# A recurrence and a routed mixture of experts: a newly searched order for five engines, smaller routing groups, and the sums of the first experts' inputs on VectorE

## The chip, the cores and the metric

One core of a Trainium2 chip. The metric is the device time of one execution in microseconds (us); lower is better. PE is TensorE, PEld its weight load, DVE is VectorE, ACT is ScalarE, POOL is GpSimd, SP is SyncE, which issues most of the DMAs.

## The reference

```
a_t  = exp(8 * sigmoid(r_gate) * log(clip(sigmoid(a_param))))
x_g  = sqrt(max(1 - a_t**2, 1e-6)) * sigmoid(i_gate) * x
h    = a_t[:, t] * h + x_g[:, t]            # over t, y[:, t] = h
tok  = y.reshape(20224, 256)
e    = argmax(tok @ w_gate)                 # 8 experts, w_gate 256 x 8
g    = softmax(tok @ w_gate)[e]
out  = g * (relu(tok @ w1[e]) @ w2[e])      # w1[e] 256 x 1024, w2[e] 1024 x 256
```

The inputs are 4 sequences of 5056 tokens of 256 channels, in float32.

## The kernel before

The 20224 tokens are 158 blocks of 128. Four blocks are a **quad**, of which there are 40 (the last has two blocks). The work of a quad is the **front**: `load` brings its gates and x (512 KB each), ACT computes `ti`, `th` (tanh), `ex` (exp), `sq` (square) and `rt` (square root), DVE computes `xi`, `b` and the recurrence `scan`. Tanh and exp on the one side and the square root on the other use different function tables of ACT, so a change of side costs a table load. Then come the **rows**: PE computes the gate logits (`lp`, `lt`) and transposes the quad to token rows (`yt`), DVE finds each row's largest magnitude (`am`) and its scale (`sc`), ACT and DVE write the row as two float16 halves (`hi`, `lw`).

Quads are put together in **groups** (`GROUPS`). Each group is routed at once: `r1` to `r6` on DVE with the two matmuls of `rk` on PE in the middle find the expert, the place of each token in its expert's stretch of a DRAM buffer, and the gate weight. `scat` on POOL writes each block there by an indirect DMA, after `fa` has put the gate weight and the token's number (`ids`) at the row's end. `fence` is a small DMA on SP behind the scatters of a group. After it the expert work is read back by `xl`: row ends (`meta`) and the transposed rows (`xT`).

The **expert work** is 90 slots, each of one expert and 256 tokens (the last 16 of 128). The first eight slots, one for each expert, are `raw`: their weights are still float32 and are prepared beside the work into float16 halves (`wm`, `wt`, `ws`, `wh`, `wl`) and written to a scratch buffer (`wr`). Their x needs the sum of its two halves: `join`, on POOL. For the first two (`PICK = 2`) x does not go through DRAM at all: DVE writes 0/1 selection matrices (`sel`) and PE gathers the rows by matmuls with them (`pick`), and ACT copies the result out (`xs`). The other 82 slots read float16 weights back (`w`, 1 MB each, left out where the expert is already in that buffer) and make six matmuls for a product in the first layer (`L1`) and three in the second (`L2`). Between lie `relu` (ACT) and `hl` (DVE). `ot` (ACT) scales the output with a factor from `fac` (POOL), and `store` (POOL) scatters it. Which expert a slot has is decided on the chip: after a group, `tab` on DVE deals out the full blocks of 256 to the next few slots.

Each engine runs its own list in order. The lists come from a planner in the same file (`Line`, `Plan`): every step is a task with an engine, an assumed duration, a priority, the tasks it follows and the buffers it takes; the planner plays them through and at each point takes the ready task of lowest priority. The priorities come from some fifteen numbers (`URGE`, `EARLY`, `PREP` and others), and `NUDGE` can add one for a single task (it is empty before).

Of the kernel before, what the change touches and what calls it, by code (L numbers as in the profile page):

```python
# [31 lines left out]
XMAX = 0.5  # L32
WTOP = 5.9e4


GROUPS = (2, 2, 2, 2, 1, 2, 3, 2, 1, 2, 2)
UNITS = 4
SINGLE = 6
BATCH = 2
PASSES = ((1, 256, 8),)  # L40

SPLIT = 8
FILL = (0.88, 0.95)
MARGIN = 1.0
LOW = 7
MOST = 6
# [7 lines left out]
PAIRS = 4  # L54
BLANK = 0
AHEAD = 8
# [3 lines left out]
PICK = 2  # L60

EARLY = 250.0

ELOAD = 90.0
WIDE = (3,)
FAR = 5.0
SWITCH = 42
PREP = (-46.0, -3.5, 112)

URGE = dict(quad=23.0, load=-22.0, norm=-37.0, rows=-11.5, hi=197.0, route=-208.0, scat=335.0, tab=-203.0,  # L70
            first=-850.0, slot=-3250.0, fac=-52.0, store=-90.0)
NUDGE = {}
BUFS = dict(r=3, i=4, x=6, rows=4, yt=2, lp=1, rank=1, tot=1, lg=4, hl=2, xT=4, hb=3, ot=9, po=1, p1=2, reg=3, x32=6)
# [8 lines left out]
class Line:  # L82

    LAT = 0.2

    def __init__(s):
        s.now, s.ids = 0.0, counter()
        s.engs = ("SP", "PE", "DVE", "ACT", "POOL")
        s.free = {e: 0.0 for e in s.engs}
        s.avail = {e: [] for e in s.engs}  # L90
        s.dma, s.act, s.calm = 0.0, "T", 0.0
        s.pools, s.uses, s.held = {}, {}, {}
        s.events, s.ops, s.made, s.done = [], [], 0, 0
# [69 lines left out]

    def run(s):
        heappush(s.events, (0.0, -1, None))
        while s.events:
# [5 lines left out]
            for e in s.engs:  # L172
# [3 lines left out]
                for k in s.avail[e]:  # L176
                    if k.ready > now + 1e-9 or not s.can_take(k.take) or k.name == "load" and s.early(*k.args):
                        continue
                    if k.name == "scat" and now < s.calm - 1e-9:
                        continue  # L180
                    p = (k.prio + (SWITCH if k.table and k.table != s.act else 0), k.seq)
# [8 lines left out]
                if k.table and k.table != s.act:  # L190
                    d += 1.3
                    s.act = k.table
                k.start = now
# [10 lines left out]
                elif k.size:  # L204
                    s.dma = max(s.dma, now + d + 0.6) + k.size
                    k.end = s.dma + 1.2
                else:
                    k.end = now + d
                heappush(s.events, (k.end, next(s.ids), k))
# [3 lines left out]
class Plan(Line):  # L213
# [14 lines left out]
    def build(s):  # L228
# [29 lines left out]
        T["blank"] = s.add("SP", 1.0, BLANK, "blank", size=7.0)  # L258
        for c in range(PASSES[0][0] + 1):
# [1156 lines left out]
```

## Time and profile before

| | us |
|---|---|
| median of three runs | 1052.61 (1051.04 to 1054.34) |
| profiled execution | 1058.75 |
| its span, first to last instruction | 1057.0 |
| PE busy in the span | 989.3 |
| DVE busy | 676.3 |
| ACT busy | 619.1 |
| POOL busy | 435.9 |

The busy time of an engine is the time in which at least one of its instructions runs; issuing a DMA is not counted for SP. [...]

### The profile page before, as it was taken

To read this page: it belongs to the slowest core of one execution; us is meant where nothing else is said; L and a number is where in the kernel's file an instruction comes from. 1 tells how busy PE (TensorE), PEld (TensorE's weight loads), DVE (VectorE), ACT (ScalarE), POOL (GpSimd) and SP (SyncE) were. 2 spreads that over 40 slices of the span, in tenths; PEclk is the share of its full clock that TensorE was granted. 3 is DMA by queue.
4 is the path that set the end of the run, shared out by engine and by line. 5 is a ranking of instruction groups with operands and counts; after the bars stand their busy time and mean duration, and the time that the engine had idled before them with its cause. 6 is when DMAs were issued, how large, how long until landed. Compare 5 with 4: busy or idle time off the path is not lost. (4 is left out here: it accounts for less than half of the span.)

```text
span 1057.0 us, 23781 instructions
## 1 busy us (share of the span) xinstructions
PE 989.3 (94%) x8854; PEld 862.1 (82%) x8854; DVE 676.3 (64%) x1387; ACT 619.1 (59%) x815; POOL 435.9 (41%) x522
## 2 busy tenths in 40 slices
PE   1469899999999999999999999999999999999997
PEld 1138688888888989888888888888888888889987
DVE  4998889887686565876847578466876473232211
ACT  8988685675746467567555765557666442222222
POOL 0264446434555335363452644525264434222222
PEclk9979899999999999999999999999999999999999
DMA  9967998899999979897899898999699994999790
GB/s 367 382 248 209 329 339 314 291 328 369 333 299 290 344 246 342 275 379 203 286 343 356 271 310 269 297 329 302 235 321 295 310 321 140 262 265 326 223 249 26
DMA packets 169347, 307.12 MB, mean 291 GB/s; under 512 B 117636, under 2 KB 122377, under 8 KB 147978
## 3 DMA queue, kind: packets, MB, share of 16 engines
q1 hardware_dynamic: 153770, 262.81, 78.4%
q0 software_dynamic: 15456, 42.74, 11.9%
q8 instruction: 70, 1.15, 0.5%
q14 instruction: 51, 0.42, 0.1%
HBM read 251.48 MB, written 65.30 MB: 300 GB/s over the span
## 5 line engine op out<-in xcount | busy, mean ns | idle before, releaser
L1129 PE MATMUL p<-xT,wt 128*128 128x256 f16 (+1 forms) x3936 | 413.6, 263 | 2.5 <-DMA wt<-wscr 2.2
L1129 PEld LDWEIGHTS <-wt 128*128 128x128 f16 x3936 | 354.9, 98 | 40.8 <-DMA wt<-wscr 2.5
L1193 POOL DMA_INDIRECT out<-ot,meta x164 | 181.1, 1104 | 400.2 <-ACT ot L1182 353.7
L1171 PE MATMUL po<-wt,hb 128*128 128x256 f16 x1184 | 322.9, 273 | 8.3 <-ACT ot L1182 6.4
L1149 DVE SCALAR_TENSOR_TENSOR hb<-p,hb 128x1024 f16<-128x1024 f32 x148 | 180.5, 1220 | 224.3 <-ACT hb L1141 207.2
L1173 PE MATMUL po<-wt,hb 128*128 128x256 f16 x1184 | 322.8, 273 | 0.1
L1172 PE MATMUL po<-wt,hb 128*128 128x256 f16 x1184 | 322.8, 273 | 0.1
L1141 ACT ACTIVATE hb<-p 128x1024 f16<-128x1024 f32 (+1 forms) x164 | 167.4, 1021 | 196.7 <-PE p L1129 167.8
L888 POOL DMA_INDIRECT buf<-rows,pi x158 | 172.4, 1091 | 47.8 <-issue 35.8
L1182 ACT ACTIVATE ot<-po,f 128x256 f32<-128x256 f32 x148 | 69.9, 472 | 172.7 <-PE po L1173 125.3
L1172 PEld LDWEIGHTS <-hb 128*128 128x128 f16 x1184 | 115.8, 98 | 21.7 <-issue 8.7
L1171 PEld LDWEIGHTS <-hb 128*128 128x128 f16 x1184 | 115.8, 98 | 16.6 <-issue 2.7
L1173 PEld LDWEIGHTS <-hb 128*128 128x128 f16 x1184 | 115.8, 98 | 13.7 <-issue 0.3
L699 DVE TENSOR_TENSOR_SCAN in_x<-in_r,in_x 128x512 f32<-128x512 f32 (+7 forms) x82 | 97.5, 1198 | 1.4
L680 DVE SCALAR_TENSOR_TENSOR in_x<-in_i,in_x 128x1024 f32<-128x1024 f32 (+1 forms) x38 | 45.7, 1203 | 48.8 <-ACT in_i L675 40.8
L1112 POOL TENSOR_SCALAR f<-meta,wt,wt 128x2 f32<-128x2 f32 (+1 forms) x82 | 37.5, 458 | 95.5 <-DMA wt<-wscr 76.6
L793 DVE SCALAR_TENSOR_TENSOR rows<-yt,fa,rows 128x256 f16<-128x256 f32 x154 | 65.4, 478 | 14.1 <-ACT rows L783 7.1
L783 ACT ACTIVATE rows<-yt,fa 128x256 f16<-128x256 f32 x154 | 61.8, 475 | 7.2 <-DVE fa L775 6.2
L1169 PE MATMUL po<-wt,hb 128*128 128x256 f32 x256 | 62.1, 392 | 1.5 <-ACT ot L1180 1.3
L664 DVE SCALAR_TENSOR_TENSOR in_x<-in_i,in_x 128x1024 f32<-128x1024 f32 (+1 forms) x38 | 46.2, 1221 | 23.5 <-ACT in_i L658 18.5
L1129 PE MATMUL p<-x,wt 128*128 128x256 f32 x256 | 59.3, 386 | 0.7 <-ACT x L928 0.7
L763 DVE TENSOR_REDUCE m<-yt 128x2 f32<-128x512 f32 x77 | 50.2, 678 | 11.2 <-PE yt L756 10.8
(126 smaller groups left out, 911.2 us busy)
## 6 DMA issues: line engine op xcount, KB each, us to landing
wt<-wscr SPq DMA_DIRECT2D x164, 1024.5 KB
in_x<-in_rix SPq DMA_DIRECT2D x39, 512.0 KB
in_r<-in_rix SPq DMA_DIRECT2D x37, 512.0 KB
in_i<-in_rix SPq DMA_DIRECT2D x37, 512.0 KB
wscr<-hl SPq DMA_DIRECT2D x16, 1024.5 KB
wt<-in_w SPq DMA_DIRECT2D x16, 1024.0 KB
buf<-pad SPq DMA_DIRECT2D x10, 272.0 KB
out<-ot,meta POOLq DMA_INDIRECT x164
```

Source lines behind the costliest of these rows:

```text
L699: V.tensor_tensor_scan(y[:, lo:hi], av[:, lo:hi], y[:, lo:hi], init, ALU.mult, ALU.add)
L793: V.scalar_tensor_tensor(r[:, 2 * p + j, D:2 * D], o["yt", p][:, j], o["sc"][:, 2 * p + j:2 * p + j + 1], r[:, 2 * p + j, 0:D], ALU.mult, ...
L888: i = G.indirect_dma_start(out=buf[:, :], out_offset=bass.IndirectOffsetOnAxis(ap=g["pi"][:, b0 + j:b0 + j + 1], axis=0), in_=rows[q]["row ...
L1129: T.matmul(pv[:, i], wv[:, wl, kk, fs], o["xT"][:, 2 * xl + kk, 0:U], start=(z == 0), stop=(z == len(seq) - 1))
L1141: A.activation(o["h"][:, gs, 0:U] if o["raw"] else o["h"][:, 0, gs, 0:U], o["p1", g], AF.Relu)
L1149: V.scalar_tensor_tensor(o["h"][:, 1, gs, 0:U], o["p1", g], 0.0, o["h"][:, 0, gs, 0:U], ALU.max, ALU.subtract)
L1169: T.matmul(dst, h[:, f, ts], wv[:, f, :], start=(f == 0), stop=(f == NF - 1))
L1171: T.matmul(dst, h[:, 0, f, ts], wv[:, 0, f, :], start=(f == 0), stop=False)
L1172: T.matmul(dst, h[:, 0, f, ts], wv[:, 1, f, :], start=False, stop=False)
L1173: T.matmul(dst, h[:, 1, f, ts], wv[:, 0, f, :], start=False, stop=(f == NF - 1))
L1182: A.activation(o["ot", j], o["po", j], AF.Copy, scale=o["f2"][:, j:j + 1])
L1193: i = G.indirect_dma_start(out=out[:, :], out_offset=bass.IndirectOffsetOnAxis(ap=o["id"][j], axis=0), in_=o["ot", j], in_offset=None, bou ...
```

## The change

The task's work is the same: 90 slots, of which 8 raw, 66 of 256 and 16 of 128 tokens. What changes:

- **The orders.** Most of the planner's numbers are new, its assumed durations are shorter, it now counts eight outstanding DMAs on each issuing queue and a slow PE at the start, and `NUDGE` has some 700 entries. So all five lists are in another order.
- **Groups.** The first groups are as before (two quads each), the later ones are of one quad: 31 groups instead of 21, and with them 31 routings and fences instead of 21, and 22 tables instead of 19.
- **One picked expert instead of two.** `sel` and the columns of `pick` are halved; seven raw slots go through DRAM and `join` instead of six.
- **`join` on DVE** instead of POOL.
- **Rows that are not picked** (quads 4 and up) scatter in blocks each led by two copies, the block's ids and its gate weights, where before two wider copies served the quad. The ids of the picked quads are copied by a task of their own (`tag`).
- The sum of `wt` alternates between two columns, `ws` uses one scale for each layer, the row buffer `inc` is held until its table is read.
- A raw slot whose weights would be read back (`BACK`) is added to the planner; with `PASSES` as it is no slot uses it.

```diff
-GROUPS = (2, 2, 2, 2, 1, 2, 3, 2, 1, 2, 2)
+GROUPS = (2, 2, 2, 2, 1, 2, 2, 1, 3, 2, 1)
-SINGLE = 6
-BATCH = 2
+SINGLE = 8
+BATCH = 1
-LOW = 7
-MOST = 6
+LOW = 9
+LOWS = 3
+MOST = 4
-BLANK = 0
-AHEAD = 8
+BLANK = 20
+AHEAD = 10
-PICK = 2
+PICK = 1
+ADDER = 'DVE'
-EARLY = 250.0
+EARLY = 580.4
-URGE = dict(quad=23.0, load=-22.0, norm=-37.0, rows=-11.5, hi=197.0, ...
+URGE = dict(quad=23.9, load=-21.4, norm=-91.8, rows=-18.2, hi=371.6, ...
-NUDGE = {}
+NUDGE = {
+"L1(0,0)": -172.8, "L1(0,1)": -110.6, "L1(1,0)": -22, ...
...
     @op
     def fa(q):
         g, b0, _ = group(q)
-        r, nb = rows[q]["rows"], plan.quads[q]
-        if plan.group_of[q] <= PASSES[0][0]:
-            for j in range(nb):
-                G.tensor_copy(r[:, j, D:D + 1], g["mx"][:, b0 + j:b0 + j + 1])
-            return
-        G.tensor_copy(r.bitcast(I32)[:, 0:nb, D + 1:PITCH], ids[:, q * QB:q * QB + nb]...)
-        G.tensor_copy(r[:, 0:nb, D:D + 1], g["mx"][:, b0:b0 + nb].unsqueeze(2))
+        for j in range(plan.quads[q]):
+            G.tensor_copy(rows[q]["rows"][:, j, D:D + 1], g["mx"][:, b0 + j:b0 + j + 1])
...
     @op
     def scat(q, j):
         g, b0, _ = group(q)
         c = plan.group_of[q]
+        if not plan.picked(q):
+            mark(q, j)
+            G.tensor_copy(rows[q]["rows"][:, j, D:D + 1], g["mx"][:, b0 + j:b0 + j + 1])
         i = G.indirect_dma_start(
...
     def join(k):
-        G.tensor_tensor(x[:, :, 0:U], o["xT"][:, 0:2, 0:U], o["xT"][:, 2:4, 0:U], ALU.add)
+            (V if ADDER == "DVE" else G).tensor_tensor(x[:, :, 0:U], o["xT"][:, 0:2, 0:U], ...)
```

ACT, from the second pair of quads' square roots to the copy of the picked x (line 928 before, 1411 after); `hb` and `in_i` are gates, `rows` the float16 rows. Before:

```order
L675 ACT_TABLE_LOAD
L675 ACTIVATE hb<-hb,quarter 128x1024
L653 ACT_TABLE_LOAD
L653 ACTIVATE hb<-hb,k_89 128x512
L669 ACTIVATE hb<-hb 128x1024
L675 ACT_TABLE_LOAD
L675 ACTIVATE hb<-hb,quarter 128x1024
L647 ACT_TABLE_LOAD
```

After:

```order
L1138 ACTIVATE hb<-hb 128x1024
L1144 ACT_TABLE_LOAD
L1144 ACTIVATE hb<-hb,quarter 128x1024
L1138 ACTIVATE hb<-hb 128x1024
L1144 ACTIVATE hb<-hb,quarter 128x1024
L1261 ACTIVATE rows<-yt,fa 128x256 x4
L1127 ACT_TABLE_LOAD
```

The two square roots of the pair stand together, with two table loads around them instead of four; ahead of the copy of the picked x ACT's list has 13 table loads before and 8 after.

DVE, behind the second group's routing (buffers numbered; `in_x` are fronts, `hl` weights in preparation, `m` magnitudes). Before:

```order
L680 SCALAR_TENSOR_TENSOR in_x_193<-in_i_190,in_x_193 128x1024
L988 SCALAR_TENSOR_TENSOR hl_573<-misc_131,wtop_121 128x2
L990 RECIPROCAL wsc_695<-hl_573 128x1
L699 SCALAR_TENSOR_TENSOR in_x_193<-in_r_231,in_x_168,in_x_193 128x512
L699 SCALAR_TENSOR_TENSOR in_x_193<-in_r_231,in_x_193 128x512
L664 SCALAR_TENSOR_TENSOR in_x_297<-in_i_204,in_x_297 128x1024
L1000 SCALAR_TENSOR_TENSOR hl_573<-wt01_137,wsc_695,hl_573 128x2048
L763 TENSOR_REDUCE m_744<-yt_705 128x2
```

After, up to the first `join` (line 1599):

```order
L1487 SCALAR_TENSOR_TENSOR hl_609<-wt10_141,wsc_661,hl_609 128x2048
L1133 SCALAR_TENSOR_TENSOR in_x_399<-in_i_422,in_x_399 128x1024
L1133 SCALAR_TENSOR_TENSOR in_x_701<-in_i_447,in_x_701 128x1024
L1475 SCALAR_TENSOR_TENSOR hl_698<-misc_133,wtop_121 128x2
L1477 RECIPROCAL wsc_747<-hl_698 128x1
L1242 TENSOR_REDUCE m_750<-yt_740 128x2
L1133 SCALAR_TENSOR_TENSOR in_x_513<-in_i_672,in_x_513 128x1024
L1242 TENSOR_REDUCE m_750<-yt_753 128x2
L1487 SCALAR_TENSOR_TENSOR hl_698<-wt00_138,wsc_747,hl_698 128x2048
L1133 SCALAR_TENSOR_TENSOR in_x_487<-in_i_694,in_x_487 128x1024
L1599 TENSOR_TENSOR x32_782<-xT_737 128x512
```

The sum for the second expert now stands in DVE's list behind fronts, rows and weight operations; before, it stood on POOL behind the scatters.

POOL, the scatter of a quad that is not picked (ids, gate weights, indirect DMA). Before:

```order
L881 COPY rows<-ids 128x4x15
L882 COPY rows<-mx 128x4
L888 DMA buf<-rows,pi 166400x272
L1193 DMA out<-ot,meta 20224x256
L888 DMA buf<-rows,pi 166400x272 x3
```

After:

```order
L1349 COPY rows<-ids 128x15
L1369 COPY rows<-mx 128x1
L1370 DMA buf<-rows,pi 166400x272
L1695 DMA out<-ot,meta 20224x256
L1349 COPY rows<-ids 128x15
L1369 COPY rows<-mx 128x1
L1370 DMA buf<-rows,pi 166400x272
```

Each block now has its own two copies; 142 blocks are scattered so.

## Rows read from the trace of the kernel before

**Rows 1.** The page's part 1: busy us (share of the span) xinstructions.

```profile
PE 989.3 (94%) x8854; PEld 862.1 (82%) x8854; DVE 676.3 (64%) x1387; ACT 619.1 (59%) x815; POOL 435.9 (41%) x522
```

**Rows 2.** Windows: from:to, length, busy PE PEld DVE ACT POOL, clock, DMA share, GB/s.

```profile
0.00:80.00 80.00, 32.97 (x176) 16.57 (x176) 61.39 (x153) 71.59 (x84) 26.62 (x49) 0.91 0.89 334
80.00:205.00 125.00, 120.28 (x610) 102.23 (x611) 109.80 (x173) 93.32 (x107) 60.92 (x55) 0.97 0.90 292
205.00:350.00 145.00, 139.08 (x1257) 120.97 (x1256) 109.52 (x242) 88.63 (x123) 71.31 (x81) 1.00 1.03 328
350.00:800.00 450.00, 449.39 (x4187) 398.17 (x4186) 306.68 (x640) 280.51 (x380) 199.43 (x234) 1.00 0.93 298
800.00:1000.00 200.00, 198.99 (x2034) 179.36 (x2032) 79.11 (x175) 72.09 (x104) 64.43 (x87) 1.00 0.88 268
1000.00:1057.00 57.00, 48.55 (x601) 44.76 (x598) 9.80 (x8) 12.92 (x18) 13.19 (x19) 0.95 0.54 151
```

**Rows 3.** Timeline of PE: start, us, line, operation [idle before, releaser].

```profile
76.13 3.62 PE L922 MATMUL p<-hb,rows 128*128 128x512 f16 x16
...
80.42 3.72 PE L1129 MATMUL p<-x,wt 128*128 128x256 f32 x16 [0.67 <-ACT x L928]
...
205.14 2.78 PE L1129 MATMUL p<-xT,wt 128*128 128x256 f16 x24
...
1027.82 4.44 PE L1129 MATMUL p<-xT,wt 128*128 128x128 f16 x48 [2.18 <-DMA wt<-wscr]
```

**Rows 4.** Timeline of ACT ahead of the first expert's matmuls.

```profile
76.54 1.28 ACT L658 ACT_TABLE_LOAD   x1
...
79.79 1.07 ACT L928 COPY x<-p 128x512 f32<-128x512 f32 x2 [0.89 <-PE p L922]
```

**Rows 5.** Timeline of DVE: end of the second group's routing, first selection.

```profile
69.14 0.20 DVE L871 RECIPROCAL mx<-mx 128x8 f32<-128x8 f32 x1
69.26 3.40 DVE L910 TENSOR_SCALAR hb<-cst,pf 128x256 f16<-128x256 f16 x16
```

**Rows 6.** Timeline of POOL and SP: last early scatter, fence, first join.

```profile
84.58 0.97 POOL L888 DMA_INDIRECT buf<-rows,pi  x1 [0.30 <-issue]
...
90.84 0.25 SPq L933 DMA_DIRECT2D fence<-buf  x1
...
96.06 1.16 POOL L1100 TENSOR_TENSOR x<-xT 128x512 f32<-128x512 f16 x1 [10.51 <-DMA xT<-buf]
```

**Rows 7.** Timelines of DVE and POOL: one weight operation twice, and a join.

```profile
76.09 2.33 DVE L1000 SCALAR_TENSOR_TENSOR hl<-wt,wsc,hl 128x2048 f16<-128x2048 f32 x1
...
98.11 3.27 DVE L1000 SCALAR_TENSOR_TENSOR hl<-wt,wsc,hl 128x2048 f16<-128x2048 f32 x1
98.08 1.15 POOL L1100 TENSOR_TENSOR x<-xT 128x512 f32<-128x512 f16 x1 [0.86 <-DMA xT<-buf]
```

**Rows 8.** Timeline of POOL: the same four copies at two places.

```profile
69.40 0.72 POOL L879 COPY rows<-mx 128x1 f32<-128x1 f32 x4 [6.91 <-DVE mx L871]
...
75.69 3.91 POOL L879 COPY rows<-mx 128x1 f32<-128x1 f32 x4
```

**Rows 9.** POOL's groups by line and form: id copies (busy us, mean ns).

```profile
L881 POOL COPY rows<-ids 128x60 int32<-128x60 int32 x35 | 13.6, 388 | 0.0
...
L786 POOL COPY rows<-ids 128x15 int32<-128x15 int32 x16 | 4.5, 326 | 8.2 <-DMA ids<-in_ids 8.2
```

**Rows 10.** DVE's groups by line and form: two operations.

```profile
L819 DVE TENSOR_TENSOR oh<-eq,pmx 128x64 f16<-128x64 f32 x17 | 8.5, 502 | 0.6
...
L664 DVE SCALAR_TENSOR_TENSOR in_x<-in_i,in_x 128x512 f32<-128x512 f32 x1 | 0.7, 691 | 0.7 <-ACT in_i L658 0.7
```

**Rows 11.** Windows in the first experts' stage, columns as above.

```profile
125.00:130.00 5.00, 3.48 (x12) 2.80 (x13) 4.83 (x11) 2.71 (x3) 0.00 (x0) 0.66 1.04 370
130.00:135.00 5.00, 5.00 (x18) 3.99 (x17) 4.33 (x8) 3.53 (x4) 0.98 (x1) 0.65 0.99 352
```

**Rows 12.** Waits of PE from 205 to 400 us: total us, times, longest.

```profile
PE po L1171 <- ACT ot L1182: 4.1, 3, 2.2
```

More of the change, by code (lines that the diff above doesn't have):

```diff
@@ L258, in build @@
         T["blank"] = s.add("SP", 1.0, BLANK, "blank", size=7.0)
+        s.parts, e = [], 0
+        for c, U, n in PASSES:
+            s.parts.append((c, U, list(range(e, e + n))))
+            e += n
         for c in range(PASSES[0][0] + 1):
@@ L370, in route @@
+        T["r3", c] = a("DVE", 0.58 * f, pr, "r3", c, after=[T["rk", c]], take=[("inc", c)], give=[("rank", c)])
+        T["r4", c] = a("DVE", 0.2 * f, pr, "r4", c, after=[T["r3", c]])
+        T["gt", c] = a("ACT", 0.2 * f, pr - 6, "gt", c, after=[T["r1", c]], table="T")
+        T["r5", c] = a("DVE", (0.45 if c <= PASSES[0][0] else 0.3) * f, pr, "r5", c, after=[T["r4", c]])
+        T["r6", c] = a("DVE", 0.7 * f, pr, "r6", c, after=[T["gt", c], T["r5", c]] + [T["sc", q] for q in g])
         sc = []
@@ L391, in route, with fenced @@
                 for k in range(PICK):
-                    T["xs", k] = a("ACT", 0.55, -210 + k, "xs", k, after=[T["pick", q]], take=[("x32", k)], give=[("p1", "pick")])
+                    T["xs", k] = a("ACT", 0.18 + 0.32 * PASSES[0][1] / 256, -210 + k, "xs", k, after=[T["pick", q]], take=[("x32", k)], give=[("p1", "pick")])
+    def fenced(s, c):
+        s.routed(c)
+        s.add("DVE", 0.01, -1e6, "drop", c, after=[s.tabbed], give=[("inc", c)])
     def routed(s, c):
@@ L432, in table @@
         k0 = len(s.slots)
[L433 to L435 removed]
+        x = s.tabbed
+        for j, d in enumerate((0.9, 0.85, 0.95)):
+            x = s.tabbed = s.add("DVE", d, pr, "tab", z, j, after=[x])
         new = []
@@ L1094, in join, with add, weights @@
     @op
+    def add(k):
+        o = slots[k]
+        x, o["xT"] = o["xT"], ps_y.tile([P, 2, D], F32, name="yt")
+        for l in range(2):
+            T.matmul(o["xT"], id16, x[:, 2 * l:2 * l + 2], start=(l == 0), stop=(l == 1))
+    @op
     def join(k):
         o = slots[k]
-        U = o["U"]
         x = work.tile([P, 2, 256], F32, name="x32", bufs=BUFS["x32"])
-        G.tensor_tensor(x[:, :, 0:U], o["xT"][:, 0:2, 0:U], o["xT"][:, 2:4, 0:U], ALU.add)
+        if ADDER == "PE":
+            A.copy(x, o["xT"])
+        else:
+            U = o["U"]
+            (V if ADDER == "DVE" else G).tensor_tensor(x[:, :, 0:U], o["xT"][:, 0:2, 0:U], o["xT"][:, 2:4, 0:U], ALU.add)
         o["xT"] = x
+    def weights(o, i):
+        return o.get("head", o)["w", i]
     @op
```

302 lines of the change are left out of this document (179 added, 123 removed), and 412 rows, old and new, of the table NUDGE.

## The prediction

> **What bounds the kernel now.** I read the busy times first, then the span cut into stages, then the list of PE at the borders of the stages, and last what PE waited for. PE is busy 989.3 of 1057.0 us [rows 1], so the time is PE's work plus the time in which PE has none. The stages [rows 2] show where that is. From 0 to 80 us PE works 33.0 us: the reader is to see that here ACT is the full engine, 71.6 of 80, and that DVE has 61.4. From 80 to 205 us, the eight float32 experts, PE has 120.3 of 125 and DVE 109.8, so DVE is a close second. From 205 to 350 us PE lacks 5.9 us while the DMA share is 1.03; from 350 to 1000 us it lacks 1.6 us of 650; in the last 57 us it lacks 8.5, of which some 4.3 follow the last matmul. The first expert's matmuls begin at 80.42 us, the first float16 ones at 205.14 [rows 3]. So there is not much to gain: the start, about 8 us within the first experts (idle and a slow clock), and about 12 us of gaps behind them.
>
> The executed work of the experts is the same: both lists hold 164 first-layer groups, the same float16 matmuls and 164 weight loads. With the reference's inputs the tables need 16 of the last small slots in both, so the conditional code for more is not entered.
>
> **The change part by part.**
>
> *The start.* ACT's list up to the copy of the picked x has 13 table loads before and 8 after, at 1.28 us each [rows 4]: 6.4 us. It has two operations over 1024 elements fewer ahead of it; two copies of 512 elements take 1.07 [rows 4], so about 2.1, and one copy instead of two, 0.5. That is 9.0 us off an engine that is busy 71.6 of the first 80 [rows 2]. On the other engines: behind the second routing, which ends at 69.34, DVE selects for 3.40 us [rows 5]; halved, that saves 1.7. The last 16 matmuls of the pick take 3.62 [rows 3]; halved in columns, 1.8. Routing to first matmul goes from 11.1 us to about 7.6. Bounds: if only this chain is shorter, 3.5 us; if ACT's 9.0 come off and its 8.4 us of waiting go as well, 17. The quads' inputs come through the same busy DMA (share 0.89 [rows 2]) behind six 1 MB weight loads, as before, so I keep a little back from the 9.0 and take **-8**: first expert at 72.4, second routing done near 64.8.
>
> *One picked expert instead of two.* Before, two experts (four times 3.72 us each by [rows 3], 30 us together) covered the way of the others through DRAM: last scatter at 84.58, fence at 90.84, first join at 96.06 [rows 6], 26.7 us behind the routing's end at 69.34 [rows 5]. Now one expert, 14.9 us and some 2 us of PE's other rows, must do it. 72.4 + 17 = 89.4; 64.8 + 26.7 + 0.7 for the join = 92.2. The scatters could be quicker, since the eight weight copies stand ahead of them in one piece. DVE's own queue ahead of the first join holds three weight operations of 2.33 [rows 7], six operations over 1024 elements and six over 512 at 0.69 [rows 10] for each 512, and small ones: about 23 us, which ends at 88 if it never waits, so the DMA way ends last. PE idles 0 to 8 us there; I take **+2**.
>
> *`join` on DVE.* Seven times 0.69 by the nearest row, an operation on 512 elements with two inputs [rows 10], is 4.8 us for DVE. But POOL's join had a price on DVE too: the same weight operation took 2.33 us alone and 3.27 with a join beside it [rows 7]. Six times 0.94 is 5.6. So I cost the move at **0** (bounds -6 and +5 us of DVE, whose spare time of 15 us in the stage [rows 2] hides it). [...]
>
> *Copies before each scatter.* 35 quads had one id copy of 0.388 [rows 9] and one of the weights; 142 blocks now have an id copy of 0.326 (the narrow form, [rows 9]) and a weight copy that takes 0.18 to 0.98, four in 0.72 or in 3.91 us [rows 8]. POOL's extra work is 50 us at the low price, and 160 us if every copy takes 0.98. POOL is busy 435.9 us [rows 1] and becomes 46 to 56% busy. What hides it: a 256-token slot takes PE 10.3 us, 96 matmuls of the 4187 in 450 us [rows 2], and in that time POOL has two stores, a factor and about two blocks. A block is 1.3 for the DMA and 0.5 to 2 for the copies. So I take **0**, and keep the upper end for the last rival.
>
> *Smaller groups.* Ten more routings of 13 small DVE operations, none dearer than 0.50 [rows 10]: under 65 us, nearer 30, and three more tables. They lie behind 205 us, where DVE is idle 35, 143 and 121 us in the three stages [rows 2]. On PE ten more pairs of matmuls with at most 64 columns; 512 columns cost 0.23 [rows 3], so 0.06 to 0.23 each: **+1**.
>
> *The orders behind 205 us.* PE waits there for ACT's output copy, at most 2.2 us at a time [rows 12], and that copy waits for a factor which needs the weights; DMA is full (1.03). Of the weight loads 30 are left out before, and by the same tables 22 now; eight more are 8 MB, 26 us of DMA at 328 GB/s [rows 2] spread over a run whose share is about 0.93. At the end a wait for weights costs 2.18 us, and the matmuls behind it run slow, 4.44 us [rows 3]. Of 11.6 us of such gaps a new order can remove all, or add some 6 more. One wait ends as another begins on a full DMA, so I take a third: **-4**. [...]
>
> The sum is -8 + 2 + 0 + 0 + 1 - 4 = -9. Against the profiled execution, 1058.75, that is 1049.75. The profiled one lay 6.1 us above the median of the runs, so against the median the forecast is 1052.61 - 9 = **1043.6 us**.
>
> **The rivals.** A difference under 0.3% (3.2 us) can't be told from none.
>
> 1. *The new order closes nearly all gaps.* PE's row from 205 to 1000 us is already almost full, which speaks for a list that can be kept full; that the DMA is full where PE waits speaks against it. Then -8, nothing for the second expert, -7 in the first experts, -11.6 behind, +1: -25.6, 1027 us.
> 2. *The start is given back.* DVE has 109.8 us of work in the first experts' stage and its list begins only some 4.5 us earlier (64.8 against 69.34), with seven joins more. If its waits, 15 us, stay, the float16 experts begin at 203 to 206 as before, and PE idles in between. Then the time is within 3 us of 1052.
> 3. *POOL's copies and DVE block each other (slower).* Six quads, 24 blocks, are scattered in the first experts' stage: 48 copies where 12 stood. At 0.33 us of DVE held per copy that is 16 us, and at 0.98 us per copy POOL's eight blocks of a group take 27 us instead of 11, so fence and tables come later. DVE's 15 us of spare time are gone from some 8 us of holding on, if it still waits as it does; from there each us goes to PE, which loses the 8 of the start and 7 more. Time 1060. For it: [rows 7, 8]. Against it: four copies beside the selection took only 0.72. [...]
>
> **How the numbers follow.** The forecast has 0.48, no gaps 0.20, given back 0.16, slower 0.16. Faster by over 0.3% is the first two, 0.68; no difference 0.16; slower 0.16. The range reaches from the full case without gaps, 1027, to within the slow one, 1058, which leaves out less than 2 in 10; the likeliest case alone is 1036 to 1049, by the bounds of the start and of the second expert.
>
> **What would show it.** In the new profile: the first expert's matmul at 69 to 76 us, 8 table loads ahead of it, a pick of half the length; PE idle for about 2 us before the second expert; the first float16 matmul near 197; ACT's share of the first 80 us no longer the largest by far. DVE's weight operation should not be stretched by a join any more, but may be by copies. PE should lack 6 to 9 us from 205 us to the last matmul. I am wrong if the first expert begins at 78 or later, if PE idles over 8 us before the second one, if the float16 work begins past 203, or if PE waits for stores or factors on POOL.

## The result and the profile after

The changed kernel takes 1063.17 us (median of four runs, 1061.44 to 1065.59) where the kernel before takes 1052.73 in the same comparison: ratio 1.0101, 95% interval 1.0074 to 1.0128. It is about 1% slower, 10.4 us, where I had forecast 9 us faster. Its profiled execution took 1065.59 us with a span of 1063.7, 6.7 us longer than the span before.

The page's part 1 of the kernel after answers to [rows 1]:

```profile
PE 989.3 (93%) x8874; PEld 869.0 (82%) x8874; DVE 693.6 (65%) x1561; ACT 617.4 (58%) x822; POOL 465.0 (44%) x726
```

PE is busy as long as before to a tenth, so the difference of the spans equals that of PE's idle time. That the two busy times agree is chance: the pick has become 7.8 us shorter (below), and the other matmuls together take as much longer. The windows of the kernel after, cut and laid out as [rows 2], say where it lies:

```profile
0.00:80.00 80.00, 33.84 (x206) 25.36 (x207) 62.23 (x144) 71.34 (x83) 26.25 (x52) 0.87 0.97 356
80.00:205.00 125.00, 113.24 (x578) 94.76 (x577) 107.36 (x180) 94.37 (x109) 46.64 (x65) 0.96 0.93 294
205.00:350.00 145.00, 139.92 (x1227) 122.06 (x1226) 112.49 (x252) 94.55 (x130) 81.43 (x126) 0.99 1.04 328
350.00:800.00 450.00, 448.42 (x4197) 396.05 (x4195) 340.46 (x863) 284.80 (x402) 233.71 (x366) 1.00 1.01 316
800.00:1000.00 200.00, 200.00 (x2019) 180.94 (x2017) 60.04 (x116) 57.93 (x82) 62.91 (x100) 1.00 0.90 259
1000.00:1063.70 63.70, 53.92 (x661) 49.84 (x658) 11.03 (x9) 14.43 (x20) 14.04 (x20) 0.94 0.49 143
```

Length less PE's busy time, stage by stage, before and after: 47.0 and 46.2; **4.7 and 11.8**; 5.9 and 5.1; 0.6 and 1.6; 1.0 and 0.0; 8.5 and 9.8. The sums are 67.7 and 74.4. In these two executions the stage from 80 to 205 us, the first experts, has taken all of it; what other executions show of the stages behind it stands under "Why the prediction was wrong". PE's timeline of the kernel after shows that stage, as [rows 3] did (at the end of a row: the idle time ahead of it, and what ended it):

```profile
71.92 8.86 PE L1631 MATMUL p<-x,wt 128*128 128x256 f32 x32 [2.55 <-ACT x L1411]
...
88.72 5.41 PE L1671 MATMUL po<-wt,hb 128*128 128x256 f32 x16 [2.03 <-ACT ot L1682]
93.97 3.62 PE L1631 MATMUL p<-x,wt 128*128 128x256 f32 x16
...
102.78 3.72 PE L1671 MATMUL po<-wt,hb 128*128 128x256 f32 x16 [1.46 <-ACT hb L1643]
108.16 1.99 PE L1671 MATMUL po<-wt,hb 128*128 128x256 f32 x8 [1.66 <-ACT ot L1684]
...
140.02 5.38 PE L1631 MATMUL p<-x,wt 128*128 128x256 f32 x16 [2.12 <-DMA wt<-in_w]
...
198.46 0.63 PE L1225 MATMUL yt<-cst,in_x 128*128 128x128 f32 x4 [2.13 <-DVE rows L1268]
...
206.03 2.78 PE L1631 MATMUL p<-xT,wt 128*128 128x256 f16 x24
```

The first expert does begin 8.5 us earlier, at 71.92 against 80.42. The second (93.97) needs no wait for its x. In between and behind, PE stops for 1.5 to 2.1 us again and again: for ACT's output copy, for the relu, for weights, for rows. Behind the waits at 88.72 and 140.02 the next 16 matmuls take 5.4 instead of 3.72 us, which is another 1.7: the granted TensorE clock, as a share of full speed, is 0.83 in the windows from 90 to 100 and from 140 to 150 us. Behind the two shorter ones, 1.46 and 1.66 us, they do not. The float16 work begins at 206.03, 0.9 us later than before.

And it begins with more left to do. PE's groups by line and form from 0 to 205 us, before:

```profile
L1129 PE MATMUL p<-x,wt 128*128 128x256 f32 x256 | 59.3, 386 | 0.7 <-ACT x L928 0.7
L1169 PE MATMUL po<-wt,hb 128*128 128x256 f32 x224 | 54.7, 394 | 1.5 <-ACT ot L1180 1.3 <-ACT ot L1182 0.2
```

and after:

```profile
L1631 PE MATMUL p<-x,wt 128*128 128x256 f32 x256 | 61.3, 397 | 4.7 <-ACT x L1411 2.5 <-DMA wt<-in_w 2.1
L1671 PE MATMUL po<-wt,hb 128*128 128x256 f32 x204 | 49.8, 396 | 6.4 <-ACT ot L1684 2.9 <-ACT ot L1682 2.0 <-ACT hb L1643 1.5
L1404 PE MATMUL p<-hb,rows 128*128 128x256 f16 x64 | 12.2, 375 | 6.0 <-DVE hb L1392 6.0
```

The pick is down from 20.0 us (486 ns for 512 columns before) to 12.2. But of the float32 matmuls of the experts 480 were done by 205 us before and 460 are now: 20 more at 0.22 us (7.17 for 32, as PE's timeline has it undisturbed) are still to come, 4.4 us. Counting these matmuls at several moments gives the course of the lead: at 90 us 35 before and 54 after, 19 ahead; at 112 us 126 and 130, 4 ahead; at 205 us 20 behind. So nearly all of the lead of 8.5 us is gone by 112 us, within the second expert. From there to 205 us another 24 matmuls, some 5 us, are lost; PE idles 6.6 of these 93 us, 3.4 before. The groups from 70 to 112 us in the kernel after show where it went:

```profile
L1631 PE MATMUL p<-x,wt 128*128 128x256 f32 x74 | 18.5, 409 | 2.5 <-ACT x L1411 2.5
L1671 PE MATMUL po<-wt,hb 128*128 128x256 f32 x56 | 14.8, 422 | 5.1 <-ACT ot L1682 2.0 <-ACT ot L1684 1.7 <-ACT hb L1643 1.5
```

Behind the first expert's start these are 5.1 us of waits and 3.4 us of slow matmuls (8.86 instead of 7.17 and 5.41 instead of 3.72). Before, one wait of 0.88 us stood there, in PE's timeline:

```profile
108.84 1.99 PE L1169 MATMUL po<-wt,hb 128*128 128x256 f32 x8 [0.88 <-ACT ot L1180]
```

That is 7.6 us more, of a lead of 8.5. (The slow matmuls are in part this execution's own: join_gpsimd has the same wait of 2.55 us ahead of its first expert, and then 7.17, not 8.86.)

The end has changed its wait, but has not become cheaper: from 1000 us on PE idles 9.8 us, 8.5 before. PE's timeline of the kernel after at 1020 us, to be read beside the last of [rows 3]:

```profile
1019.52 0.61 PE L1631 MATMUL p<-xT,wt 128*128 128x128 f16 x8 [0.30 <-PEq L1821]
1023.90 4.42 PE L1631 MATMUL p<-xT,wt 128*128 128x128 f16 x40 [3.77 <-issue]
```

The wait for weights, 2.18 us, is gone. In its place PE stands still for 3.77 us in the middle of a group, eight matmuls behind a branch (line 1821, around the code for more small slots), and waits for nothing that the profile shows. The 40 matmuls behind it run slow, 4.42 us; the granted clock is 0.62 from 1025 to 1030 us.

### The profile page after: what moved, and what is told of

The parts are those of the page before. It is cut to its first block, busy times and chain, and to the rows that moved or that the text cites. A ratio compares the mean times of both kernels' runs of the same rounds, so it can differ in the third digit from the quotient of the medians.

```text
span 1063.7 us, 24237 instructions
## 1 busy us (share of the span) xinstructions
PE 989.3 (93%) x8874; PEld 869.0 (82%) x8874; DVE 693.6 (65%) x1561; ACT 617.4 (58%) x822; POOL 465.0 (44%) x726
## 3 DMA queue, kind: packets, MB, share of 16 engines
q1 hardware_dynamic: 155998, 271.47, 82.4%
## 4 chain that ended last, share of the span: by engine, by line
PE 72%; DMA 8%; ACT 6%; issue 6%; DVE 4%; POOL 2%; SPq 1%; POOLq 0%; ACTq 0%; DVEq 0%
PE p L1631 33%; PE po L1673 11%; PE po L1675 10%; PE po L1674 10%; PE yt L1225 3%; PE po L1671 2%; DMA wt<-in_w 2%; PE misc L1187 2%; DMA in_x<-in_rix 2%; DMA out<-ot,meta 1%; POOL out L1695 1%; DMA wscr<-hl 1%; DMA xT<-buf 1%; DVE in_x L1133 1%; ACT in_r L1122 1%
## 5 line engine op out<-in xcount | busy, mean ns | idle before, releaser
L1695 POOL DMA_INDIRECT out<-ot,meta x164 | 170.9, 1042 | 342.8 <-ACT ot L1684 288.8
L1370 POOL DMA_INDIRECT buf<-rows,pi x158 | 178.6, 1130 | 57.4 <-POOL rows L1369 37.8
L1261 ACT ACTIVATE rows<-yt,fa 128x256 f16<-128x256 f32 x154 | 62.0, 476 | 28.1 <-DVE fa L1254 17.4
L1149 DVE SCALAR_TENSOR_TENSOR in_x<-in_i,in_x 128x1024 f32<-128x1024 f32 (+1 forms) x38 | 45.5, 1200 | 36.2 <-ACT in_i L1144 36.1
L1631 PEld LDWEIGHTS p<-x,wt 128*128 128x128 f32 x256 | 50.3, 199 | 13.3 <-issue 2.9
L1242 DVE TENSOR_REDUCE m<-yt 128x2 f32<-128x512 f32 x77 | 51.3, 681 | 14.7 <-PE yt L1225 13.1
```

The lines of the kernel that those rows point to most:

```text
L1370: i = G.indirect_dma_start(out=buf[:, :], out_offset=bass.IndirectOffsetOnAxis(ap=g["pi"][:, b0 + j:b0 + j + 1], axis=0), in_=rows[q]["row ...
L1631: T.matmul(pv[:, i], wv[:, wl, kk, fs], o["xT"][:, 2 * xl + kk, 0:U], start=(z == 0), stop=(z == len(seq) - 1))
L1695: i = G.indirect_dma_start(out=out[:, :], out_offset=bass.IndirectOffsetOnAxis(ap=o["id"][j], axis=0), in_=o["ot", j], in_offset=None, bou ...
```

## The experiments

Each run is given as its ratio to the kernel before on the same chip, with the 95% interval; the changed kernel has 1.0101 (1.0074 to 1.0128). "Idle" is PE's idle time from 80 to 205 us, 4.7 before and 11.8 after. In moves of one task, `X behind Y` means that task X now stands right behind Y in its engine's list; nothing else moves.

**Parts undone: copies, join, nudges, the picked expert.** First my third rival, that GpSimd's 142 pairs of small copies are the cost. In the changed kernel:

```diff
         if not plan.picked(q):
-            mark(q, j)
-            G.tensor_copy(rows[q]["rows"][:, j, D:D + 1], g["mx"][:, b0 + j:b0 + j + 1])
+            r, nb = rows[q]["rows"], plan.quads[q]
+            if "led" not in rows[q]:
+                rows[q]["led"] = True
+                G.tensor_copy(r.bitcast(I32)[:, 0:nb, D + 1:PITCH], ids[:, q * QB:q * QB + nb]...)
+                G.tensor_copy(r[:, 0:nb, D:D + 1], g["mx"][:, b0:b0 + nb].unsqueeze(2))
```

> The changed kernel with its lists kept, but a quad's ids and gate weights are copied once, in two wide copies ahead of its first scatter, as before the change. Theory A (the gain of the start is lost because ACT's list is full behind the first expert, so evictions come late): no difference, within 3 us of the changed kernel's 1063. Theory B (my slower rival: GpSimd's small copies hold up DVE and the scatters): the loss goes away, 1050 to 1056, and PE's idle time from 80 to 205 us falls from 11.8 to below 7.

Measured: 1.0188 (1.0134 to 1.0242), slower and not faster; idle 11.4. The float16 work begins at 202.85, but behind 205 us PE now waits for weights:

```profile
PE p L1634 <- DMA wt<-wscr: 3.8, 1, 3.8
```

So the copies are not what the first experts wait for.

```diff
-            (V if ADDER == "DVE" else G).tensor_tensor(x[:, :, 0:U], o["xT"][:, 0:2, 0:U], ...)
+            G.tensor_tensor(x[:, :, 0:U], o["xT"][:, 0:2, 0:U], ...)
```

> The changed kernel with its lists kept, but the seven sums of the raw experts' x on GpSimd again. Theory A: DVE loses 4.9 us of work in the first experts' stage, which it gets back as stretched weight operations; 1060 to 1065. Theory C (DVE is the engine that is too full in that stage): 3 to 5 us faster, 1058 to 1060, with the wait for rows at 198 us gone.

Measured: 1.0121 (1.0062 to 1.0181), no difference from the changed kernel; idle 10.0. DVE's weight operation, by groups, and then two of DVE's rows that ran beside joins:

```profile
L1487 DVE SCALAR_TENSOR_TENSOR hl<-wt,wsc,hl 128x2048 f16<-128x2048 f32 x16 | 37.3, 2343 | 0.4 <-ACT hl L1482 0.4
```

```profile
92.94 1.12 DVE L1253 TENSOR_SCALAR sc<-m 128x4 f32<-128x4 f32 x1
...
116.57 1.50 DVE L1253 TENSOR_SCALAR sc<-m 128x4 f32<-128x4 f32 x1
```

No weight operation is stretched here, but none ran beside a join either (the joins lie at 92.2 to 95.2, 105.4 to 107.0 and 113.6 to 118.0 us). The operation of these two rows took 0.16 and 0.17 us in the kernel after, at 92.45 and 116.37 us, and takes 1.12 and 1.50 here. So DVE lost about 1 us at a time beside two of the joins, and the time of the kernel doesn't show it.

```diff
-NUDGE = {
-"L1(0,0)": -172.8, "L1(0,1)": -110.6, ...
+NUDGE = {}
```

> The changed kernel planned without its 700 nudges, everything else the same. If the nudges hold the lists together: 5 to 20 us slower than the changed kernel, 1068 to 1083, with more idle time of PE behind 205 us. If they only shift single steps: within 5 us of 1063.

Measured: 1.0451 (1.0401 to 1.0501), some 37 us above the changed kernel; the first expert begins at 84.80 and the float16 work at 246.51. The changed numbers alone make a worse order; the single nudges hold it together.

In the kernel before, with one picked expert and the lists that its planner makes of that:

```diff
-PICK = 2
+PICK = 1
```

> The kernel before, planned by its own numbers, with one picked expert instead of two and nothing else changed. Theory A: the pick is halved, the first expert starts 2 to 4 us earlier, the table loads stay; PE then idles 5 to 10 us ahead of the second expert, since its planner gives the other experts' way no earlier place: 1052 to 1060. If the single pick is worth what I put on it: 1048 to 1050.

Measured: 1.0132 (1.0084 to 1.0180). This is the change's start without its other parts: first expert at 74.02, idle 5.6, float16 at 196.09, 9 us earlier than before. Then it is lost: from 205 to 350 us PE idles 17.4 us, by the waits

```profile
PE p L1129 <- DMA wt<-wscr: 5.5, 1, 5.5
...
PE po L1171 <- DMA wt<-wscr: 2.6, 1, 2.6
PE misc L830 <- DVE lg L742: 2.6, 1, 2.6
```

An early start can thus be carried through the first experts, by another order, and is then paid back where the float16 weights have to come. The reverse, the changed kernel with two picked experts (`PICK = 2`):

> The changed kernel, planned anew with two picked experts, its nudges and all else kept (the nudges were found for one). If the single pick is what costs (PE waits for the second expert's x, which comes at 93 us): idle time from 80 to 110 us below 2.5, the first expert 2 to 3 us later, end 1055 to 1063. If the nudges fit one pick only: slower than 1065, with new waits behind 110 us.

Measured: 1.1032 (1.0994 to 1.1070). The 700 nudges fit one list only; with another set of tasks they cost 100 us, so nothing follows on the second picked expert itself.

**The waits one by one.** Are the 2-us waits each a fault of one place in a list? On SP `xl(7)` behind `raw(4,0)` (SP stands from 101.4 to 109.5 us ahead of it, and the DMA share falls to 0.25); on ACT the weight operation `wh(0,0)` behind the output copy `ot(0,0)`, and tanh, exp and square of quad 8 behind `hi(4,1)`:

```diff
+MOVES = (("xl(7,)", "raw(4,0)"),)                            # sp_order
+MOVES = (("wh(0,0)", "ot(0,0)"), ("th((8,(0,)),)", "hi(4,1)"), # act_order
+         ("ex((8,(0,)),0)", "th((8,(0,)),)"), ("sq((8,(0,)),)", "ex((8,(0,)),0)"))
```

> The changed kernel with one step moved on SP's list: the read-back of the last raw expert's x, which waits from 101.4 to 109.5 us for a buffer that the sums on VectorE free late, now stands behind the next two raw weight loads. Theory D (the DMA sets the pace, and this wait, in which its share is 0.25, lost the lead in bytes that the earlier start had given): the DMA share of 100 to 110 us rises above 0.7, PE's wait for raw weights at 140 us (2.1 us and a slow clock) goes, the first float16 matmul comes 3 to 6 us earlier and the end 3 to 8: 1055 to 1060. Theory A (ACT): the wait at 140 goes and the end is within 3 us of 1063.

> The changed kernel with four steps moved on ACT's list: a weight half of 2 us behind the first expert's output copy, and tanh, exp and square of a later front behind the evictions and rows up to 110 us. Theory A: PE's three waits for ACT between 86 and 108 us (2.0, 1.5 and 1.7) fall to below 1 in sum and with them the slow stretch behind the first, the first float16 matmul comes 5 to 8 us earlier and the end 5 to 8: 1055 to 1058. Theory D: these waits fall too, but the time is not kept, since DMA has to bring the same bytes: end within 3 us of 1063.

> Both moves together. Theory A: as with ACT's alone, 1055 to 1058. Theory D: as with SP's alone, 1055 to 1060, PE's lead of the first experts' stage being lost again between 205 and 350 us. If either is only worth something with the other: 1048 to 1055.

Measured: 1.0154 (1.0118 to 1.0190), 1.0115 (1.0080 to 1.0150) and, with both, 1.0171 (1.0127 to 1.0216). Each move does what it says and none gains. With SP's move the DMA share from 100 to 110 us rises from 0.25 to 0.61 and the wait for weights at 140 us is gone. With ACT's the three waits for ACT shrink to 0.56 us together, and PE's timeline has others in their place:

```profile
87.37 3.72 PE L1682 MATMUL po<-wt,hb 128*128 128x256 f32 x16
93.44 5.38 PE L1642 MATMUL p<-x,wt 128*128 128x256 f32 x16 [2.35 <-issue]
...
110.67 5.38 PE L1642 MATMUL p<-x,wt 128*128 128x256 f32 x16 [2.02 <-issue]
```

The first of them is for the x of the second expert. DVE's timeline of act_order has its join:

```profile
92.65 0.68 DVE L1610 TENSOR_TENSOR x<-xT 128x512 f32<-128x512 f16 x1
```

It ends at 93.33. In the changed kernel DVE's join runs from 91.85 for 0.69 us, to 92.54, and PE comes to it only at 93.97; the waits for ACT had used up the time. Idle is 11.7 with SP's move and 10.2 with ACT's. With both moves the clock is 1.00 from 80 to 1000 us, PE's busy time falls to 982.8, and idle rises to 14.4.

PE's and ACT's lists together (`yt(9,0)`, the logits `lp` of quads 10 and 11, and `yt(9,1)` behind `L2(6,0,0)` on PE, with ACT's moves):

> The changed kernel with ACT's four moves, and on PE's list the two transposes of the tenth quad and its gate logits moved behind two matmul groups of the seventh expert, so that PE has work where it waited 2.1 us for DVE at 196 us. If the list's order alone makes the gaps: idle time of 160 to 205 us down from 4.0 to below 2, first float16 matmul before 202, end 1057 to 1061. If DVE, which runs late there behind the writes of the weights, is the cause: the wait comes back at the next transposes or evictions, end within 3 us of 1063.

This one computes something else: ACT's copy of the logits of quads 10 and 11 stands ahead of the matmuls that make them, so these two quads are routed by older logits. Its time, 1.0115 (1.0076 to 1.0154), carries no verdict, and the run is inconclusive.

**Bandwidth.** The changed kernel loads 8.7 MB more on SP's queue (271.47 against 262.81). In the kernel before, eight weight loads more are made unconditional, 8 MB:

```diff
-            cond = None if was is None or was[1] else o["er"] != was[0]
+            cond = None if was is None or was[1] or k in (17, 18, 24, 34) else o["er"] != was[0]
```

> The kernel before with eight more weight loads of 1 MB: slots 17, 18, 24 and 34 load both halves even where they hold them already, as many loads more as the changed kernel has. Theory D: 26 us of DMA at 328 GB/s, six of the loads in the stage whose share is 1.03, so 5 to 20 us slower, 1058 to 1073. Theory A: the DMA has room, within 3 us of 1053.

Measured: 1.0009 (0.9983 to 1.0035): the loads cost nothing that can be told.

**Does a us at the start reach the end?** In either kernel, 34 calls of a float32 matmul more on PE ahead of the first expert, into a result that is then overwritten:

```diff
+        if (k, g) == (0, 0):
+            for _ in range(34):
+                T.matmul(pv[:, 0], wv[:, 0, 0, 0:P], o["xT"][:, 0, 0:U], start=True, stop=True)
```

> The same 34 matmuls in the kernel before, whose first experts' stage has only 4.7 us of idle time. Theory F: 7 to 8 us slower, 1060 to 1062. Theory E for this kernel too (what comes after is set by the other engines): under 4 us slower, below 1057.

> The changed kernel with 34 float32 matmuls of 0.23 us, 7.9 us of idle work for PE, ahead of the first expert's first group; they are written over, and everything else is kept. Theory E (the early start is worth nothing in this order, because the x of the second expert and the evictions by ACT come when they come, and PE only waits for them): within 3 us of the changed kernel's 1063, PE's idle time from 80 to 205 us down from 11.8 to 5 to 8. Theory F (PE's own work carries every delay to the end): 1069 to 1072.

The delay was larger than I had meant. Each call became two matmuls, and PE's timeline of late_start_before has all 68 of them:

```profile
79.86 14.94 PE L1128 MATMUL p<-x,wt 128*128 128x256 f32 x68 [0.68 <-ACT x L928]
94.64 3.62 PE L1132 MATMUL p<-x,wt 128*128 128x256 f32 x16
```

So 14.8 us were put in, not 7.9. Measured: 1.0088 (1.0059 to 1.0116) before, 9.3 us; and 1.0211 (1.0172 to 1.0251) after, some 11.6 us above the changed kernel. The kernel before takes back about a third: idle from 80 to 205 us falls from 4.7 to 1.7, and the float16 work begins only 8.4 us later (213.51). So a late us of PE is carried to the end for the most part, not in full. In the changed kernel idle falls to 7.1, as theory E had it, but the time follows the delay for the most part all the same. Its first waits come back, later. PE's timeline of late_start_after:

```profile
103.43 5.41 PE L1674 MATMUL po<-wt,hb 128*128 128x256 f32 x16 [2.02 <-ACT ot L1685]
...
122.03 1.99 PE L1674 MATMUL po<-wt,hb 128*128 128x256 f32 x8 [1.66 <-ACT ot L1687]
```

The waits of 2.03 and 1.66 us at 88.72 and 108.16 have moved with PE by 14.7 and 13.9 us and kept their length. So these two are not set by data that comes at a given time: they are in the order of the lists. ACT's timeline of the kernel after shows the first:

```profile
86.43 1.99 ACT L1482 ACTIVATE hl<-wt,wsc 128x2048 f16<-128x2048 f32 x1
88.32 0.35 ACT L1682 COPY ot<-po 128x256 f32<-128x256 f32 x1
```

A 2-us weight operation stands ahead of the 0.35-us copy for which PE waits.

**What makes the start early?** I had put it to ACT's table loads. In the kernel before, `rt((2,(0,1)))` behind `sq((3,(0,1)))`, so that two pairs' square roots stand together, with two table loads fewer:

```diff
+MOVES = (("rt((2,(0,1)),)", "sq((3,(0,1)),)"),)
```

> The kernel before with one step moved: the square root of the third quad behind the squares of the fourth, which saves two of the 13 table loads ahead of the first expert, 2.57 us of ACT, and nothing else. If the start's 2.6 us carry to the end (theory F): 1050 to 1051. If they are given back in the first experts' stage (theory E): within 1.5 us of 1053.

Measured: 1.0004 (0.9978 to 1.0029); the first expert at 80.87, not earlier. ACT only waits longer for the logits, 5.24 us instead of 2.58. DVE's timeline there shows why:

```profile
45.53 3.30 DVE L921 TENSOR_SCALAR hb<-cst,pf 128x256 f16<-128x256 f16 x16
48.75 1.21 DVE L691 SCALAR_TENSOR_TENSOR in_x<-hb,in_x 128x1024 f32<-128x1024 f32 x1
50.00 2.46 DVE L710 TENSOR_TENSOR_SCAN in_x<-hb,in_x 128x512 f32<-128x512 f32 x2
```

The 16 selections of the first group stand ahead of the recurrence that the second group needs. The changed kernel has eight of them, in two lots; its recurrence there is done at 51.58 us, 55.65 before. The rows' low halves (`lw`), which stood ahead of the second routing, stand within it. So that routing starts on DVE at 55.96, 64.90 before, and ends at 64.48, 69.34 before. One run bears on this from the other side: one_picked has 11 table loads ahead of its copy of the picked x, where the kernel before has 13 and the changed one 8, and its first expert starts 6.4 us earlier than before all the same (74.02).

**Is DVE the engine that holds the first experts back?** In the changed kernel the weight operation `wl` becomes a fill with zeros (the low halves of the weights are left out), which takes 16 times 1.4 us = 23 us from DVE (0.91 us each instead of 2.34):

```diff
-        V.scalar_tensor_tensor(o["t"][:, 2 * F:4 * F], o["w"], o["s"], o["t"][:, 0:2 * F], ...)
+        V.memset(o["t"].bitcast(F32)[:, F:2 * F], 0.0)
```

> The changed kernel, lists kept, with the low half of each prepared weight left out: VectorE fills it with zeros instead of computing it (sixteen operations of 2.35 us become fills of at most 1.1, 20 us of VectorE less up to 210 us; PE's matmuls are the same). Theory I (behind the start VectorE, with its share of the fronts and of the weights, sets when rows, sums and routings are done, so PE's lead can't be used): idle time of PE from 80 to 280 us from 15.3 to below 9, 5 to 10 us faster, 1053 to 1058. If PE's gaps are fixed by the lists of the other engines: within 3 us of 1063.

Measured: 1.0090 (1.0062 to 1.0118). DVE has 98.3 us from 80 to 205 instead of 107.4, and PE's waits are the same ones:

```profile
89.11 3.72 PE L1671 MATMUL po<-wt,hb 128*128 128x256 f32 x16 [2.02 <-ACT ot L1682]
...
102.33 3.72 PE L1671 MATMUL po<-wt,hb 128*128 128x256 f32 x16 [2.31 <-ACT hb L1643]
...
107.71 1.99 PE L1671 MATMUL po<-wt,hb 128*128 128x256 f32 x8 [1.66 <-ACT ot L1684]
```

Idle is 10.9. The float16 work begins 5.4 us earlier, at 200.64, and the end is the same: from 350 to 1000 us PE idles 5.9 instead of 1.6. (Such a difference in one execution says little: with the same lists up to that point it began at 205.14 in the kernel before and at 200.72 in tail_before, below.) So these waits are not made by DVE's amount of work, and what was won ahead of 205 us was lost behind it.

**The pause near the end.** In the changed kernel, 34 float16 matmuls more in the first pick, at 35 us, shift all later code of PE; then the same with ACT's moves from above and two on DVE (`wl(0,0)` behind `join(1)`, `wm(7,1)` behind `lw(8,1)`):

```diff
+        for _ in range(34 if q == 0 else 0):
+            T.matmul(st["pick"][:, 0, 0:PICK * PASSES[0][1]], r[:, 0, 0:P], ...)
```

> The changed kernel with 34 float16 matmuls more at the first pick, at 35 us, where PE waits anyway; they are written over, and they shift the rest of PE's program by 68 instructions. Theory G (3.8 us of the changed kernel's tail, within a group of matmuls and behind a branch, depend on where PE's instructions lie, as the run with the late start suggests, in which they were gone): the pause goes, the slow stretch behind it too, 4 to 6 us faster, 1057 to 1059. Otherwise (the pause waits for data): within 1 us of 1063, the pause in place.

> The same padding, ACT's four moves, and two moves on DVE: the sum for the second expert ahead of a weight operation of 2.3 us, and the rows of the ninth quad ahead of a reduction of 2.3 us. Theory H (the loss is the sum of such waits in the lists and of the slow clock behind them): idle time from 80 to 205 us from 11.8 to below 7, the tail as with the padding, 1050 to 1055. If a removed wait is only followed by the next: 1057 to 1060, as with the padding alone.

Measured: 1.0071 (1.0044 to 1.0098) and 1.0064 (1.0036 to 1.0091). The pause is gone; PE's timeline of the padded kernel has all 48 at once, in 2.84 us:

```profile
1021.14 2.84 PE L1633 MATMUL p<-xT,wt 128*128 128x128 f16 x48 [0.30 <-PEq L1823]
```

PE's idle time behind 1000 us falls from 9.8 to 6.0, though the pad itself makes the first expert 2 us later. The ratios lie 3 us under the changed kernel's, with intervals that overlap. In the second run idle from 80 to 205 us is still 11.6: a wait removed is followed by the next.

**A version that beats both.** In the kernel before, on SP, the weights of slot 87 are asked for right behind its slot number, ahead of those of slot 85's second layer:

```diff
+MOVES = (("w(85,1)", "w(86,0)"), ("w(87,0)", "slot(87,)"), ("w(85,1)", "w(87,0)"))
```

> The kernel before with two moves on SP's list in its last 50 us: the weight loads of slot 87 ahead of those second halves of slots 85 and 86 which wait for a buffer. If SP's queue is the cause of PE's wait at 1025.6 us (2.2 us and a slow clock behind it): the wait goes, 2 to 4 us faster, 1049 to 1051. If the transfer itself is the limit there (DMA share about 1): no difference.

> The kernel before with the two moves on SP's list at the end and the square root of the third quad moved, which saves two table loads. If each is worth what it showed alone (3.5 us and nothing): 1049 to 1050, the same as with the tail alone. If the table loads add something in this version: below 1048.

Measured: 0.9967 (0.9947 to 0.9988) and, with the pair of square roots from above, 0.9962 (0.9937 to 0.9988). The wait of 2.18 us and the slow 4.44 us behind it [rows 3] are gone, and the granted clock is 1.00 from 1020 to 1030 us:

```profile
1022.93 2.84 PE L1140 MATMUL p<-xT,wt 128*128 128x128 f16 x48
```

Some 3.5 us, a third of a per cent, by two moved loads: the only gain of this study. It is a gain of the median; beside tail_before the fastest of 23 executions of the kernel before took 1050.85 us, and the fastest of 12 with the moves 1052.04.

## Why the prediction was wrong

**The start, -8: right in size, its cause not settled.** First expert at 71.92 (forecast 72.4), second routing done at 64.48 (64.8), eight table loads ahead, pick halved. But the 9.0 us that I took off ACT are not shown to have done it. Two of the five table loads, taken off alone (pairs_before), gave nothing, and one_picked won 6.4 of the 8.5 us with 11 loads. DVE's order is the other candidate: its second routing began 8.9 us earlier. That is read from the timelines; no run put DVE's order alone into the kernel before.

**One picked expert, +2: the mechanism held, the block was mis-sized.** I had 72.4 + 17 = 89.4 for the first expert against 92.2 for the next x. The x came at 92.5. The first expert's stretch took 22 us, 71.92 to 93.97, by PE's own wait of 2 us and the slow clock at its start and end (8.86 instead of 7.17, 5.41 instead of 3.72). Where the wait for ACT was taken away (act_order), PE waited 2.35 us for this x, as the term had it.

**Idle and slow clock within the first experts, for which the sum has no term: the step that failed.** Idle there went from 4.7 to 11.8 us [rows 2]. I had shown that the change reorders all five lists, and costed only the operations that it adds and removes in this stage, not the order in which ACT serves PE there. The order decides the first waits: late_start_after moved PE by 14.7 us, and two of them moved along unchanged; lean_vector took DVE's work away, and they stayed; act_order took them away, and the next ones, for x from DVE, stood behind them. The size of the step is firm: in eight variants that keep the changed kernel's order on PE idle was 10.0 to 14.4 us, in four that keep the order before 4.3 to 4.8 (the two late starts, 7.1 and 1.7, apart). That it makes up the whole loss is not shown, since no run that took single waits away gained clear of the noise.

**Join on DVE, 0, and POOL's copies, 0: held.** Moving the join back and widening the copies gained nothing. The stretch of 0.94 us [rows 7], from which I priced the join, was not tried again, since in join_gpsimd no weight operation met a join; two other DVE operations took 1.12 and 1.50 us beside joins, instead of 0.16 and 0.17. One reading was wrong: the 2.33 us of [rows 7] that I called "alone" had POOL's four long copies beside it, 75.69 to 79.60 us [rows 8].

**Groups, +1: no run undoes them.** PE's timeline of the kernel after shows what a pair of routing matmuls takes from the others, 0.06 us from the first one's start to that of the next work:

```profile
215.60 0.20 PE L1305 MATMUL misc<-oh,ones 128*128 128x64 f16 x1
215.63 0.20 PE L1306 MATMUL misc<-oh,umat 128*128 128x64 f16 x1
215.66 5.41 PE L1631 MATMUL p<-xT,wt 128*128 128x256 f16 x48
```

By these rows ten more pairs would be 0.6 us, an estimate. Seen from 205 us on, the 6.7 us of the spans are 6.2 us more work of PE left (842.3 against 836.0, of which the 20 float32 matmuls are 4.4) and 0.5 us more idle time.

**The orders behind 205 us, -4: this failed too.** Idle from 205 us to the end went from 16.0 to 16.5 in the profiled executions. The wait for weights at the end did go, as I hoped; a pause of 3.77 us in the same place took its room, with the same slow matmuls behind it. And the other runs say that the new order loses behind 205 us. Windows of tail_before, and then of lean_vector, columns as in [rows 2]:

```profile
205.00:350.00 145.00, 137.93 (x1234) 118.60 (x1233) 106.65 (x236) 86.66 (x119) 68.48 (x78) 0.99 1.02 322
350.00:1000.00 650.00, 649.39 (x6244) 579.35 (x6242) 385.24 (x813) 353.07 (x485) 268.25 (x321) 1.00 0.91 289
```

```profile
205.00:350.00 145.00, 139.49 (x1246) 121.82 (x1245) 111.18 (x248) 94.45 (x128) 77.17 (x126) 1.00 1.06 343
350.00:1000.00 650.00, 644.10 (x6172) 572.64 (x6171) 394.81 (x973) 339.77 (x477) 293.94 (x458) 1.00 0.95 294
```

From 205 to 1000 us PE lacks 7.7 us there and 11.4 here. In the nine variants with the changed kernel's order on PE it lacks 9.6 to 11.8; in the five with the order before 3.7 to 7.7, and 7.5 in that kernel's own profile. Only the changed kernel's own profile, 6.7, lies outside its row. So behind 205 us the new order cost, by these runs, some 4 us more of idle time, where I had it gain 4.

**The rivals.** The -7 that the first has for the first experts' stage is shown by no run: idle there was 10.0 us or more wherever PE kept the new order, the late start's 7.1 apart. The second, "the start is given back", had the float16 work at 203 to 206 and PE idle in between; that is what happened (206.03), but it ended at "no change", and left out that PE would by then also be behind in float32 work. The third had sign and size, 1060, by a mechanism that wide_copies refutes: its 0.33 us of DVE held for each copy is shown by no run, and with two wide copies for a quad idle was 11.4 us, against 11.8, and the ratio 1.0188. Of my conditions for being wrong, idle over 8 us "before the second one" was not met, the float16 work past 203 was.

**What stays open.** The medians differ by 10.4 us and the profiled executions by 6.8: the profiled one of the kernel before lay 6.1 above its runs' median, that of the changed kernel 2.4. The account by stages explains the 6.7 us of the spans. For the rest, the idle time from 205 to 1000 us told above is the likeliest place, but no run took it away. Which of the 2-us waits would have to be mended together to keep the lead isn't settled: moves of one to six tasks changed which wait it was, and idle from 80 to 205 us stayed at 10 to 14 us.

## What to carry to other kernels

A list order that starts earlier is not a gain until each later engine's list has been read for who stands ahead of the operation that PE needs next; two waits that lay in the list's order here, of 2.03 and 1.66 us, moved with PE by 14.7 and 13.9 us and kept their length (2.02 and 1.66). Of a delay of PE by 14.8 us 9.3 reached the end in the kernel before, and some 11.6 of the like delay in the changed kernel; of the start's lead of 8.5 us nothing did. Don't read a cause from one execution's stages alone: the variants that share the order showed idle time behind 205 us that the profiled pair hid.

## What the runs showed of the hardware

- A gap of PE of about 2 us in the float32 work is followed by slow matmuls in some executions and not in others, at the same place of the same list. Behind the gap of 2.03 us at 88.72 the next 16 matmuls took 5.41 us; behind one of 2.02 us there they took 3.72 in lean_vector and in wide_copies. With the moves on ACT and SP (sp_and_act), gaps of 2.35 and 2.47 us were followed by 3.69, the clock is 1.00 from 80 to 1000 us, and PE's busy time falls by 6.5 us, from 989.3 to 982.8. In join_gpsimd the 16 behind a gap of 1.62 us took 6.34. So such a gap cost its own length here, or 1.7 us more, and 2.6 in that run; what decides it stays open.
- PE stopped for 3.0 to 4.0 us near the end of some runs without waiting for any engine or transfer that the profile shows. PE's waits from 800 us on have this in the changed kernel (3.77 us), in seven variants of it (3.2 to 4.0) and in one_picked (3.0). In the changed kernel and in lean_vector the timelines show the place, eight matmuls behind the branch: the eight start at 1019.52 and 1018.29 us, and pauses of 3.77 and 3.94 us follow. The pause is not there in the two padded kernels, nor in late_start_after, where PE has 68 matmuls more ahead of that branch, nor in two_picked_after and the kernel before; in no_nudges there is a wait of 5.2 us at the branch itself. So with 34 float16 matmuls more (padded_after) or 68 float32 ones (late_start_after) ahead of the branch the pause was gone; what makes it is not shown.
- Eight more loads of 1 MB in a kernel whose DMA share is 0.88 to 1.03 up to 1000 us [rows 2] cost 0.9 us, with an interval of -1.8 to +3.7.
